# Two 128-byte spacers ahead of hh and hl, and two 128-row tiles in place of a transposed product for experts with 768 slots

## The chip, the cores and the metric

One NeuronCore of a Trainium2 chip runs the whole program. The metric is device time in microseconds (us), the median of several runs of the same program on the same inputs. A lower number is better.

## The reference

An attention layer (4 batches, 8 heads, 768 positions, head size 64; each query sees 8 global keys and the last 96 local ones) feeds a mixture of experts over N = 3072 tokens of width D = 512:

```python
logits = x @ w_gate
noisy = logits + np.log1p(np.exp(x @ w_noise)) * noise
top2 = two largest of noisy, weights by softmax over the two
for e in range(8):
    for k in range(2):
        mask = top2[:, k] == e
        h = np.maximum(x[mask] @ w1[e], 0.0)       # 512 -> 1024
        out[mask] += top2_w[mask, k, None] * (h @ w2[e])   # 1024 -> 512
```

Each expert therefore takes some 768 of the 6144 token-expert pairs, with two dense products per pair. All of it is float32.

## The kernel before

The program has two halves. The first (about 190 us) is the attention with the gate and the routing of tokens; the change does not reach it. The second is the experts, one after another, in the order of their token counts. Expert number e (0 to 7) has `CAPS[e]` slots: 812, 812, 804, 792, 780, 768, 768, 768. The first `CA = 512` slots of an expert are called part 0 here, the remaining 300, 292, 280, 268 or 256 are part 1.

A float32 product is made from three products of the faster type float32r: every operand is split into a high part and a low part (`xh`/`xl`, `w1h`/`w1l`, `w2h`/`w2l`, `hh`/`hl`), and high·high, high·low and low·high are added up in PSUM. For one expert the steps are:

- `up(e, c, f)` (L841): for part c and each of the 8 blocks f of 128 hidden units, 12 matmuls (4 blocks of the 512 inputs, three products each). The weights w1 stand still in the array, the tokens x move: 512 columns for part 0, 256 to 300 for part 1. ScalarE then writes `hh` with a Relu (L845) and VectorE writes `hl` (L846).
- `down(e, t)` (L868): for each of the 4 tiles t of 128 slots of part 0, 24 matmuls (8 blocks f, three products). Here 128 columns of hh or hl stand still, and a row of 512 columns of w2 moves; the result has slots as rows and goes straight to `put`, which scales it on ScalarE (L852) and adds it to the output by a scattered DMA that GpSimd issues (L853).
- `down_t(e, d)` (L879): part 1 is done the other way round, because its length is not a multiple of 128. For each of 4 blocks d of the outputs, 24 matmuls with w2 standing still and the 256 to 300 slots of part 1 moving. The result is transposed, so it goes to `yt` (L882, L884), and
- `back(e, t)` (L892) transposes it with 4 matmuls for every 128 slots, before `put`. The `back` steps of expert e are issued inside `up` of expert e + 1, behind the blocks f = 0, 1, 2; those of the last expert stand behind its tiles 0, 1, 2.

Beside these steps stand, for the next expert, `gather` (L180, fetches 128 token rows by an indirect DMA), `turn` (L230, 4 transposing matmuls for such a tile, then copies to xh and xl) and `split` (L158, L159, ScalarE and VectorE cut w1 into its parts). The order is written by hand. In the stage of the products with w2, the list `steps + steps_t` (4 `down`, then 4 `down_t`) is run through, and behind step j come split j and turn j of the next expert. For the last expert the list is `steps_t + steps`.

The tiles of the pool `mc` lie behind one another in each partition of SBUF: w2h and w2l (16384 bytes each), xh1 and xl1 (4 rows of 1200 bytes each), then hh in two tiles (part 0: 8 rows of 2048 bytes, part 1: 8 rows of 1200), hl in two such tiles, and yt. By these sizes hh begins 42368 bytes behind w2h, which is 384 more than a multiple of 512, and hl begins 68352 behind it, 256 more than a multiple of 512. In the pool `wts`, w1h, w1l, xh and xl of part 0 lie whole multiples of 512 bytes apart.

Of the kernel before, what the change touches and what calls it, by code (L numbers as in the profile page):

```python
# [10 lines left out]
F32 = mybir.dt.float32  # L11
# [5 lines left out]
AF = mybir.ActivationFunctionType  # L17
# [3 lines left out]
P = 128  # L21
NP = 96
TA = 4
TB = 3
CA = TA * P
# [3 lines left out]
CAPS = [812, 812, 804, 792, 780, 768, 768, 768]  # L29
# [5 lines left out]
def tile_local_global_attention_then_moe(  # L35
# [13 lines left out]
    nc = tc.nc  # L49
# [100 lines left out]
    def split(e, x, j, eng=nc.vector):  # L150

        t = raw[x, e, j // 4]
        if x == 1:
            t = t[:, :, (j % 4) * P:(j % 4 + 1) * P]
            hi, lo = (y[:, :, j * P:(j + 1) * P] for y in (w1h, w1l))
        else:
            t, hi, lo = t[:, j % 4], w2h[:, j], w2l[:, j]
        nc.scalar.activation(hi, t, AF.Copy)  # L158
        eng.tensor_sub(lo, t, hi.bitcast(F32))  # L159
        if j % 4 == 3 and (e or x == 2):  # L160
            load_w()
# [3 lines left out]
    def tiles(e):  # L165
        return -(-CAPS[e] // P)
# [657 lines left out]
    with ExitStack() as mctx:  # L824
        mc = mctx.enter_context(tc.tile_pool(name="mc", bufs=1))
        mw = mctx.enter_context(tc.tile_pool(name="mw", bufs=2))
        w2h = mc.tile([P, FC, Dm], FR, name="w2h")
        w2l = mc.tile([P, FC, Dm], FR, name="w2l")
        xh.append(mc.tile([P, KC, CB], FR, name="xh1"))
        xl.append(mc.tile([P, KC, CB], FR, name="xl1"))  # L830
        hh = [mc.tile([P, FC, n], FR, name=f"hh{n}") for n in (CA, CB)]
        hl = [mc.tile([P, FC, n], FR, name=f"hl{n}") for n in (CA, CB)]
        yt = mc.tile([P, KC, CB], F32, name="yt")
        def up(e, c, f, between=None):
            m = CAPS[e] - CA if c else CA
            ps = bank("sc" if f % 2 else "at")[:, :m]
            fs = slice(f * P, (f + 1) * P)
            n = 0
            for k in range(KC):
                for w, x in ((w1h, xh), (w1h, xl), (w1l, xh)):  # L840
                    nc.tensor.matmul(ps, w[:, k, fs], x[c][:, k, :m], start=n == 0, stop=n == 3 * KC - 1)  # L841
                    n += 1
                    if between and n % 3 == 0:
                        between()
            nc.scalar.activation(hh[c][:, f, :m], ps, AF.Relu)  # L845
            nc.vector.scalar_tensor_tensor(hl[c][:, f, :m], ps, 0.0, hh[c][:, f, :m].bitcast(F32),  # L846
                                           op0=OP.max, op1=OP.subtract)

        def put(e, t, ps):
            r, g = rows(e, t)  # L850
            y = mw.tile([r.shape[0], Dm], F32, name="y")
            nc.scalar.activation(y, ps, AF.Copy, scale=g)  # L852
            ins = nc.gpsimd.indirect_dma_start(  # L853
                out=out, out_offset=bass.IndirectOffsetOnAxis(ap=r, axis=0),
                in_=y, in_offset=None, bounds_check=N + DUMP - 1, oob_is_err=True, compute_op=OP.add)
            for o in added[e]:
                tc.declare_no_dep(ins.ins, o.ins, reason="an expert's tokens are all different")
            added[e].append(ins)

        added = [[] for _ in range(E)]  # L860

        def down(e, t):
            ps = bank("av")
            cols = slice(t * P, (t + 1) * P)
            n = 0
            for f in range(FC):
                for x, w in ((hh, w2h), (hh, w2l), (hl, w2h)):
                    nc.tensor.matmul(ps, x[0][:, f, cols], w[:, f], start=n == 0, stop=n == 3 * FC - 1)  # L868
                    n += 1
            put(e, t, ps)  # L870

        def down_t(e, d):
            m = CAPS[e] - CA
            ps = bank("av")[:, :m]
            cols = slice(d * P, (d + 1) * P)
            n = 0
            for f in range(FC):
                for w, x in ((w2h, hh), (w2h, hl), (w2l, hh)):
                    nc.tensor.matmul(ps, w[:, f, cols], x[1][:, f, :m], start=n == 0, stop=n == 3 * FC - 1)  # L879
                    n += 1  # L880
            if d % 2:
                nc.vector.tensor_copy(yt[:, d, :m], ps)  # L882
            else:
                nc.scalar.activation(yt[:, d, :m], ps, AF.Copy)  # L884

        def back(e, t):
            m = min(P, CAPS[e] - CA - t * P)
            if m <= 0:
                return
            ps = spare_bank()[:m]  # L890
            for d in range(KC):
                nc.tensor.transpose(ps[:, d * P:(d + 1) * P], yt[:, d, t * P:t * P + m], ident)  # L892
            put(e, TA + t, ps)

        late, last = pending
        slots = {
            0: [(late, 33)], 1: [gate_t, (late, 36)], 2: [(late, 39)], 3: [gate_l, (late, 42)],
            4: [], 5: [gate_s, (late, 45)], 6: [(last, 2)], 7: [(late, 48)],  # L900
            8: [(last, 5)], 9: [(last, 7)], 10: [(late, 52), (last, 8)], 11: [(last, 9)],
            12: [(last, 12)], 13: [(late, 54), (last, 13)], 14: [(last, 16)], 15: [(last, 18)],
            16: [(last, 20)], 17: [(last, 22)], 18: [(last, 24)], 19: [(last, 27)],
            20: [(last, 31)], 21: [(late, 57)], 22: [(last, 34)], 23: [(last, 37)],
            24: [(last, 39)], 25: [(last, 42)], 26: [(late, 61)], 27: [(last, 45)],
            28: [(last, 48)], 29: [(late, 99), split], 30: [split], 31: [(last, 52)],
        }
        slot, parts = [0], [0]

        def ahead():  # L910
            for x in slots[slot[0]]:
                if x is split:
                    split(0, 2, parts[0])
                    parts[0] += 1
                elif isinstance(x, tuple):
                    x[0].upto(x[1])
                elif windowed:
                    x(NT - 1)
            slot[0] += 1

        for f in range(FC):
            if NZ + f < (DUMP + N) // P // 2:
                zero_out(NZ + f)
            up(0, 0, f, ahead)
        while parts[0] < FC:
            split(0, 2, parts[0])
            parts[0] += 1
        for x in pending:
            x.upto(99)
        for t in range(TB):  # L930
            gather(0, TA + t)
        rank()
        ranked[0] = None
        load_w(held[0])
        for t in range(TA - 1):
            down(0, t)
        for t in range(TB):
            turn(0, TA + t, bank("sc") if t == TB - 1 else None)
        for t in range(3):
            gather(1, t)  # L940
        down(0, TA - 1)
        for e in range(E):
            last = e + 1 == E
            for c in range(2):
                if c or e:
                    for f in range(FC):
                        up(e, c, f)
                        if f % 2 and e:
                            split(e, 2, c * 4 + f // 2)
                        if c == 0 and f < TB:  # L950
                            back(e - 1, f)
                        if e == 0 and f % 2 and f < 6:
                            turn(1, f // 2)
                            gather(1, 3 + f // 2)
                if e and not last:
                    for t in range(3 * c, 3 + 2 * c):
                        gather(e + 1, t)
            steps = [(down, t) for t in range(TA)]
            steps_t = [(down_t, d) for d in range(KC)]
            if e == 0:  # L960
                for j in range(KC):
                    down_t(0, j)
                    if j == 0:
                        gather(1, 6)
                    turn(1, 3 + j)
                    split(1, 1, 2 * j)
                    split(1, 1, 2 * j + 1)
                continue
            for j, (f, t) in enumerate(steps_t + steps if last else steps + steps_t):
                f(e, t)  # L970
                if not last:
                    split(e + 1, 1, j)
                    if j < TA + TB:
                        turn(e + 1, j)
                        if j < 2:
                            gather(e + 1, 5 + j)
                elif j in (KC, KC + 1, KC + 2):
                    back(e, j - KC)


# [107 lines left out]
```

## Time and profile before

| | |
|---|---|
| median of 3 runs | 793.47 us (792.6 to 795.06) |
| the profiled execution: its own time | 789.53 us |
| its span, first to last instruction | 787.8 us |
| mean granted TensorE clock | 0.996 |
| TensorE matmuls busy | 771.5 us, 98% of the span, 5673 instructions |
| VectorE, ScalarE, GpSimd busy | 42%, 42%, 24% |

Matmuls are pipelined: one that the profile gives 0.39 us overlaps the next, so the time that a stream of them takes is read from their starts. Where the text speaks of a pace, it is the distance between two starts. A weight load stands in the profile as an instruction of its own, beside the matmul before it.

### The profile page before, as it was taken

How to read it: one execution, taken by the hardware profiler on the slowest of the kernel's cores; microseconds unless marked ns; L12 is line 12 of the kernel's file. 1: busy time of each engine (PE TensorE's matmuls, PEld its weight loads, DVE VectorE, ACT ScalarE, POOL GpSimd, SP SyncE). 2: the span in 40 equal slices, each digit the busy share in tenths (PEclk: the TensorE clock that was granted, in tenths of full speed). 3: DMA queues.
4: the chain of work that ended last, by engine and by line, in shares of the span. 5: the costliest groups of instructions: out<-in, count | busy, mean ns of one | idle time of the engine just before them, and what ended most of it. 6: DMA issues, size and time to landing. Idle time of an engine off the chain costs nothing.

```text
span 787.8 us, 14898 instructions
## 1 busy us (share of the span) xinstructions
PE 771.5 (98%) x5673; PEld 680.9 (86%) x5673; DVE 329.9 (42%) x1215; ACT 332.7 (42%) x726; POOL 192.3 (24%) x222
## 2 busy tenths in 40 slices
PE   7999999999999999999999999999999999999994
PEld 6989989898879989898888889898989889898983
DVE  6557566758853433233323422342334234233400
ACT  6778777765223433233333323342333323233310
POOL 2003431452035050404122321402051221211022
PEclk9999999999999999999999999999999999999998
DMA  8789675744256163344444434434453454432024
GB/s 267 241 271 315 191 204 168 220 147 151 104 156 175 56 150 108 57 126 97 117 84 103 129 83 93 108 95 97 104 123 109 64 136 122 94 81 27 2 28 58
DMA packets 58786, 99.67 MB, mean 127 GB/s; under 512 B 5076, under 2 KB 17492, under 8 KB 58704
## 3 DMA queue, kind: packets, MB, share of 16 engines
q1 hardware_dynamic: 47440, 72.79, 28.8%
q0 software_dynamic: 11264, 25.83, 18.2%
q8 instruction: 47, 0.77, 0.4%
q14 instruction: 35, 0.29, 0.1%
HBM read 71.01 MB, written 27.59 MB: 125 GB/s over the span
## 4 chain that ended last, share of the span: by engine, by line
PE 63%; issue 28%; POOL 6%; DMA 1%; POOLq 0%; DVE 0%; ACT 0%; SPq 0%
PE av L868 11%; PE sc L841 10%; PE at L841 10%; PE av L661 9%; PE av L879 7%; PE at L641 6%; PE sc L613 5%; POOL out_dram L853 4%; POOL xg L180 2%; PE m L252 1%; PE m L260 1%; PE m L230 1%; PE lg L230 1%; PE lg L426 1%; DMA out_dram<-y,ids 1%
## 5 line engine op out<-in xcount | busy, mean ns | idle before, releaser
L853 POOL DMA_INDIRECT out_dram<-y,ids x53 | 83.1, 1567 | 405.1 <-ACT y L852 404.1
L868 PE MATMUL av<-w2h,hh 128*128 128x512 f32 x256 | 102.6, 401 | 0.0
L868 PE MATMUL av<-w2h,hl 128*128 128x512 f32 x256 | 101.5, 396 | 0.0
L868 PE MATMUL av<-w2l,hh 128*128 128x512 f32 x256 | 101.2, 395 | 0.0
L159 DVE TENSOR_TENSOR w1l<-raw,w1h 128x512 fp32r<-128x512 f32 x56 | 38.3, 689 | 144.0 <-ACT w1h L158 144.0
L841 PE MATMUL sc<-xh,w1h 128*128 128x512 f32 (+5 forms) x256 | 88.3, 345 | 0.0
L841 PE MATMUL at<-xh,w1h 128*128 128x512 f32 (+5 forms) x256 | 88.3, 345 | 0.0
L841 PE MATMUL at<-xl,w1h 128*128 128x512 f32 (+5 forms) x256 | 87.1, 340 | 0.1
L841 PE MATMUL sc<-xh,w1l 128*128 128x512 f32 (+5 forms) x256 | 87.1, 340 | 0.0
L841 PE MATMUL at<-xh,w1l 128*128 128x512 f32 (+5 forms) x256 | 87.1, 340 | 0.0
L841 PE MATMUL sc<-xl,w1h 128*128 128x512 f32 (+5 forms) x256 | 87.0, 340 | 0.0
L846 DVE SCALAR_TENSOR_TENSOR hl<-sc,hh 128x512 fp32r<-128x512 f32 (+5 forms) x64 | 36.3, 568 | 97.0 <-ACT hh L845 97.0
L879 PE MATMUL av<-hh,w2h 128*128 128x256 f32 (+4 forms) x256 | 76.1, 297 | 0.0
L629 ACT ACTIVATE a<-ns,mx 128x168 f32<-128x168 f32 (+1 forms) x192 | 71.9, 422 | 6.4 <-POOL a L543 4.2
L879 PE MATMUL av<-hh,w2l 128*128 128x256 f32 (+4 forms) x256 | 74.1, 290 | 0.0
L879 PE MATMUL av<-hl,w2h 128*128 128x256 f32 (+4 forms) x256 | 74.1, 290 | 0.0
L845 ACT ACTIVATE hh<-sc 128x512 fp32r<-128x512 f32 (+5 forms) x64 | 32.0, 500 | 99.8 <-PE sc L841 99.8
L852 ACT ACTIVATE y<-av,tab 128x512 f32<-128x512 f32 x28 | 19.2, 687 | 127.2 <-issue 106.4
L180 POOL DMA_INDIRECT xg<-xd,ids x53 | 56.5, 1066 | 59.9 <-DVE place L200 38.7
L661 PE MATMUL av<-vs,at 128*128 128x65 f32 x384 | 70.9, 273 | 0.0
L845 ACT ACTIVATE hh<-at 128x512 fp32r<-128x512 f32 (+5 forms) x64 | 32.0, 500 | 86.9 <-PE at L841 86.8
L643 ACT ACTIVATE at<-at 128x512 f32<-128x512 f32 (+1 forms) x96 | 53.6, 558 | 29.6 <-PE at L641 29.2
(163 smaller groups left out, 1572.3 us busy)
## 6 DMA issues: line engine op xcount, KB each, us to landing
raw<-in_w SPq DMA_DIRECT2D x32, 1024.0 KB, 5.3
out_dram<-zero SPq DMA_DIRECT2D x14, 512.0 KB, 5.6
vs<-in_v SPq DMA_DIRECT2D x24, 260.0 KB, 4.0
qbuf<-in_q SPq DMA_DIRECT2D x24, 256.0 KB, 5.5
xd<-xr SPq DMA_DIRECT2D x24, 256.0 KB, 2.5
ks<-in_k SPq DMA_DIRECT2D x20, 272.0 KB, 4.3
vp<-in_v SPq DMA_DIRECT2D x20, 195.0 KB, 4.8
ks<-in_k SPq DMA_DIRECT2D x4, 464.0 KB
```

Source lines behind the costliest of these rows:

```text
L159: eng.tensor_sub(lo, t, hi.bitcast(F32))
L180: nc.gpsimd.indirect_dma_start(out=xg[e, t], out_offset=None, in_=xd[:n], in_offset=bass.IndirectOffsetOnAxis(ap=r, axis=0), bounds_check= ...
L613: nc.tensor.matmul(SC[n + x][y * Q:(y + 1) * Q, s], qs[b, j][r, 2 * i0 + s, u + y], ks[b, j][r, u + y, k0:k0 + w], start=True, stop=True, ...
L629: nc.scalar.activation(A[n][:, s, c:c + w], ns[:, s, :w], AF.Exp, bias=mx[:, s:s + 1], scale=-1.0)
L641: nc.tensor.transpose(p4[:, :, c, s * Q:(s + 1) * Q], x[:, s, a:a + P], ident)
L643: nc.scalar.activation(AT[n], ps, AF.Copy)
L661: nc.tensor.matmul(ps[:, h % 4], a[:kk, y * w + c0:y * w + c0 + P], t[:kk, c], start=kk < P or not i, stop=kk == P)
L841: nc.tensor.matmul(ps, w[:, k, fs], x[c][:, k, :m], start=n == 0, stop=n == 3 * KC - 1)
L845: nc.scalar.activation(hh[c][:, f, :m], ps, AF.Relu)
L853: ins = nc.gpsimd.indirect_dma_start(out=out, out_offset=bass.IndirectOffsetOnAxis(ap=r, axis=0), in_=y, in_offset=None, bounds_check=N + ...
L868: nc.tensor.matmul(ps, x[0][:, f, cols], w[:, f], start=n == 0, stop=n == 3 * FC - 1)
L879: nc.tensor.matmul(ps, w[:, f, cols], x[1][:, f, :m], start=n == 0, stop=n == 3 * FC - 1)
```

## The change

Two tiles of 32 float32 (128 bytes in each partition) are allocated ahead of hh and ahead of hl and never used. They move hh by 128 bytes and hl, yt and y by 256. By the sizes above, hh then begins 42496 bytes behind w2h and hl 68608, both whole multiples of 512.

For an expert whose part 1 is a whole number of 128-slot tiles (`whole_tiles`: experts 5, 6 and 7, with 256 slots there), hh and hl of part 1 are written and read with rows of 256 floats (1024 bytes) in place of 300 (`second`), `down` does two more tiles (t = 4, 5) with these as the standing operand, and `down_t` and `back` are left out. The splits and turns of the next expert are spread over the six steps that remain.

```diff
+        mc.tile([P, 32], F32, name="pad0")
         hh = [mc.tile([P, FC, n], FR, name=f"hh{n}") for n in (CA, CB)]
+        mc.tile([P, 32], F32, name="pad1")
         hl = [mc.tile([P, FC, n], FR, name=f"hl{n}") for n in (CA, CB)]
...
-            nc.scalar.activation(hh[c][:, f, :m], ps, AF.Relu)
+            hi, lo = (second(x[c], e) if c else x[c] for x in (hh, hl))
+            nc.scalar.activation(hi[:, f, :m], ps, AF.Relu)
...
+        def whole_tiles(e):
+            return (CAPS[e] - CA) % P == 0
+        def second(x, e):
+            if not whole_tiles(e):
+                return x
+            m = CAPS[e] - CA
+            return x.rearrange("p f t -> p (f t)")[:, :FC * m].rearrange("p (f t) -> p f t", f=FC)
...
         def down(e, t):
             ps = bank("av")
-            cols = slice(t * P, (t + 1) * P)
+            c, a = (0, t * P) if t < TA else (1, (t - TA) * P)
+            cols = slice(a, a + P)
+            hi, lo = (second(x[c], e) if c else x[c] for x in (hh, hl))
             n = 0
             for f in range(FC):
-                for x, w in ((hh, w2h), (hh, w2l), (hl, w2h)):
-                    nc.tensor.matmul(ps, x[0][:, f, cols], w[:, f], start=n == 0, stop=n == 3 * FC - 1)
+                for x, w in ((hi, w2h), (hi, w2l), (lo, w2h)):
+                    nc.tensor.matmul(ps, x[:, f, cols], w[:, f], start=n == 0, stop=n == 3 * FC - 1)
...
-            if m <= 0:
+            if m <= 0 or whole_tiles(e):
                 return
...
+            if whole_tiles(e):
+                steps, steps_t = [(down, t) for t in range(tiles(e))], []
...
-                    split(e + 1, 1, j)
-                    if j < TA + TB:
-                        turn(e + 1, j)
-                        if j < 2:
-                            gather(e + 1, 5 + j)
+                    while parts * len(steps) < FC * (j + 1):
+                        split(e + 1, 1, parts)
+                        turn(e + 1, parts)
+                        if parts < 2:
+                            gather(e + 1, 5 + parts)
+                        parts += 1
```

On TensorE, in the w2 stage of expert 5, the end of tile 3 and what follows it read before (hh_3633 and hl_3635 are part 0, hh_3634 and hl_3636 part 1; xg is a gathered tile of the next expert):

```order
L868 MATMUL av<-w2l,hh_3633 128x512
L868 MATMUL av<-w2h,hl_3635 128x512
L230 MATMUL m<-ident,xg 128x128 x4
L879 MATMUL av<-hh_3634,w2h 128x256
L879 MATMUL av<-hl_3636,w2h 128x256
L879 MATMUL av<-hh_3634,w2l 128x256
```

and in the changed program (hh_3634 and hl_3637 are part 0 there, hh_3635 and hl_3638 part 1):

```order
L884 MATMUL av<-w2l,hh_3634 128x512
L884 MATMUL av<-w2h,hl_3637 128x512
L230 MATMUL lg<-ident,xg 128x128 x4
L230 MATMUL m<-ident,xg 128x128 x4
L884 MATMUL av<-w2h,hh_3635 128x512
L884 MATMUL av<-w2l,hh_3635 128x512
L884 MATMUL av<-w2h,hl_3638 128x512
```

Two turns now stand together, and the products that follow have 512 moving columns; there are 48 of them in place of 96 with 256 columns.

On TensorE again, in `up` of expert 6, at the border of blocks f = 0 and f = 1, before:

```order
L841 MATMUL at<-xl_99,w1h 128x512
L841 MATMUL at<-xh_98,w1l 128x512
L892 MATMUL lg<-ident,yt 128x128 x4
L841 MATMUL sc<-xh_98,w1h 128x512
L841 MATMUL sc<-xl_99,w1h 128x512
```

and in the changed program:

```order
L843 MATMUL at<-xl_99,w1h 128x512
L843 MATMUL at<-xh_98,w1l 128x512
L843 MATMUL sc<-xh_98,w1h 128x512
L843 MATMUL sc<-xl_99,w1h 128x512
L843 MATMUL sc<-xh_98,w1l 128x512
```

The four transposes of `back` are gone from there, and from behind the next block too.

On ScalarE, from tile 3 of expert 5 (its y) to the start of `up` of expert 6 (hh_3633 there), before:

```order
L852 ACTIVATE y<-av,tab 128x512
L158 ACTIVATE w1h<-raw 128x4x128
L232 ACTIVATE xh_98<-m 128x4x128
L884 ACTIVATE yt<-av 128x256
L158 ACTIVATE w1h<-raw 128x4x128
L232 ACTIVATE xh_3631<-lg 128x4x128
L158 ACTIVATE w1h<-raw 128x4x128
L232 ACTIVATE xh_3631<-m 128x4x128
L884 ACTIVATE yt<-av 128x256
L158 ACTIVATE w1h<-raw 128x4x128 x2
L845 ACTIVATE hh_3633<-at 128x512
L852 ACTIVATE y<-lg,tab 128x512
```

and in the changed program:

```order
L855 ACTIVATE y<-av,tab 128x512
L158 ACTIVATE w1h<-raw 128x4x128
L232 ACTIVATE xh_3631<-lg 128x4x128
L158 ACTIVATE w1h<-raw 128x4x128
L232 ACTIVATE xh_3631<-m 128x4x128
L855 ACTIVATE y<-av,tab 128x512
L158 ACTIVATE w1h<-raw 128x4x128
L855 ACTIVATE y<-av,tab 128x512
L158 ACTIVATE w1h<-raw 128x4x128
L848 ACTIVATE hh_3634<-at 128x512
L848 ACTIVATE hh_3634<-sc 128x512
```

The copies to yt and the y of `back` are replaced by the y of tiles 4 and 5; the turns of the next expert end one step after tile 3 in place of two.

## Rows read from the trace of the kernel before

**Rows 1.** Busy time by engine in the expert half (240 to 776.5 us); granted clock, DMA.

```profile
core 0: us, PE busy (x) PEld busy (x) DVE busy (x) ACT busy (x) POOL busy (x), PEclk, DMA share, GB/s
240.00:776.50 536.50, 536.50 (x3158) 475.39 (x3156) 175.46 (x308) 177.76 (x343) 125.53 (x95) 1.00 0.40 93
```

**Rows 2.** TensorE groups by line and shape, two of them: count, busy, mean.

```profile
L868 PE MATMUL av<-w2h,hh 128*128 128x512 f32 x256 | 102.6, 401 | 0.0
...
L879 PE MATMUL av<-hh,w2h 128*128 128x256 f32 x96 | 27.4, 286 | 0.0
```

**Rows 3.** Timeline of TensorE (start us, length us, what), `up` of expert 1, part 0.

```profile
286.86 0.39 PE L841 MATMUL sc<-xh,w1h 128*128 128x512 f32 x1
...
292.30 0.39 PE L841 MATMUL sc<-xh,w1h 128*128 128x512 f32 x1
```

**Rows 4.** Timeline of TensorE, `down` of expert 0, first matmuls of tiles 1 and 2.

```profile
223.83 0.39 PE L868 MATMUL av<-w2h,hh 128*128 128x512 f32 x1
...
229.43 0.39 PE L868 MATMUL av<-w2h,hh 128*128 128x512 f32 x1
```

**Rows 5.** Timeline of TensorE, `up` of part 1: expert 1 (300 columns), expert 6 (256).

```profile
295.02 0.30 PE L841 MATMUL at<-xh,w1h 128*128 128x300 f32 x1
...
308.26 0.39 PE L868 MATMUL av<-w2h,hh 128*128 128x512 f32 x1
...
660.48 0.28 PE L841 MATMUL at<-xh,w1h 128*128 128x256 f32 x1
...
671.78 0.40 PE L868 MATMUL av<-w2h,hh 128*128 128x512 f32 x1
```

**Rows 6.** Timeline of TensorE, w2 stage of expert 5, to the start of expert 6.

```profile
601.43 0.40 PE L868 MATMUL av<-w2h,hh 128*128 128x512 f32 x1
...
607.02 0.60 PE L230 MATMUL lg<-ident,xg 128*128 128x128 f32 x4
...
613.41 0.48 PE L868 MATMUL av<-w2h,hh 128*128 128x512 f32 x1
...
619.09 0.60 PE L230 MATMUL lg<-ident,xg 128*128 128x128 f32 x4
619.44 0.48 PE L868 MATMUL av<-w2h,hh 128*128 128x512 f32 x1
...
637.72 0.40 PE L841 MATMUL at<-xh,w1h 128*128 128x512 f32 x1
```

**Rows 7.** Timeline of TensorE, `up` of expert 7, blocks f = 2 and f = 4.

```profile
714.39 0.47 PE L841 MATMUL at<-xh,w1h 128*128 128x512 f32 x1
...
719.95 0.39 PE L841 MATMUL at<-xh,w1h 128*128 128x512 f32 x1
```

**Rows 8.** Timeline of TensorE, `up` of expert 6, blocks f = 0 and f = 3.

```profile
640.49 0.60 PE L892 MATMUL lg<-ident,yt 128*128 128x128 f32 x4
...
646.88 0.39 PE L841 MATMUL sc<-xh,w1h 128*128 128x512 f32 x1
```

**Rows 9.** Timeline of TensorE, w2 stage of expert 7, first to last matmul.

```profile
742.14 0.28 PE L879 MATMUL av<-hh,w2h 128*128 128x256 f32 x1
...
753.39 0.39 PE L868 MATMUL av<-w2h,hh 128*128 128x512 f32 x1
...
776.43 0.40 PE L868 MATMUL av<-w2h,hl 128*128 128x512 f32 x1
```

**Rows 10.** Timeline of all engines, the end of the program.

```profile
776.91 0.69 ACT L852 ACTIVATE y<-av,tab 128x512 f32<-128x512 f32 x1 [4.87 <-PE av L868]
777.87 1.57 POOL L853 DMA_INDIRECT out_dram<-y,ids  x1 [3.99 <-ACT y L852]
```

**Rows 11.** Instructions that write xg, 560 to 720 us: the gathers, their landing.

```profile
DMA to landing us min/median/max: 3.5/3.7/4.3
```

**Rows 12.** Timeline of TensorE, expert 5, two slow neighbours within the first tile.

```profile
603.51 0.40 PE L868 MATMUL av<-w2h,hh 128*128 128x512 f32 x1
...
603.99 0.39 PE L868 MATMUL av<-w2h,hl 128*128 128x512 f32 x1
```

More of the change, by code (lines that the diff above doesn't have):

```diff
@@ L844, in up @@
                         between()
-            nc.scalar.activation(hh[c][:, f, :m], ps, AF.Relu)
-            nc.vector.scalar_tensor_tensor(hl[c][:, f, :m], ps, 0.0, hh[c][:, f, :m].bitcast(F32),
+            hi, lo = (second(x[c], e) if c else x[c] for x in (hh, hl))
+            nc.scalar.activation(hi[:, f, :m], ps, AF.Relu)
+            nc.vector.scalar_tensor_tensor(lo[:, f, :m], ps, 0.0, hi[:, f, :m].bitcast(F32),
                                            op0=OP.max, op1=OP.subtract)
@@ L968, in tile_local_global_attention_then_moe @@
                 continue
-            for j, (f, t) in enumerate(steps_t + steps if last else steps + steps_t):
+            if whole_tiles(e):
+                steps, steps_t = [(down, t) for t in range(tiles(e))], []
+            steps = steps_t + steps if last else steps + steps_t
+            parts = 0
+            for j, (f, t) in enumerate(steps):
                 f(e, t)
                 if not last:
-                    split(e + 1, 1, j)
-                    if j < TA + TB:
-                        turn(e + 1, j)
-                        if j < 2:
-                            gather(e + 1, 5 + j)
-                elif j in (KC, KC + 1, KC + 2):
+                    while parts * len(steps) < FC * (j + 1):
[4 more added lines that the diff above has]
+                        parts += 1
+                elif steps_t and j in (KC, KC + 1, KC + 2):
                     back(e, j - KC)
```

## The prediction

> **What bounds the kernel.** I read the busy times of the expert half first, then the starts of TensorE's matmuls. In the 536.5 us from 240 to 776.5 TensorE is busy for all 536.50, at a granted clock of 1.00, while VectorE and ScalarE work a third of that and the DMA engines are at 0.40 [rows 1]. So in this half time goes only where the stream of matmuls gets shorter, and whatever leaves VectorE, ScalarE or GpSimd is worth nothing by itself. The attention half is not touched.
>
> A matmul's length in the profile (401 ns for the 256 of one `down` product [rows 2]) is no pace, since neighbours overlap. The starts give it. In `up` of part 0, 24 matmuls of 512 columns take 292.30 - 286.86 = 5.44 us, 226.7 ns each [rows 3]. In `down`, 24 matmuls of 512 columns take 229.43 - 223.83 = 5.60 us, 233.3 ns each [rows 4]. The shape is the same, and so is the pattern of three products (two matmuls with the high weights, one with the low, moving high, low, high), and neither stream has a gap. What differs is where the operands lie. In `up`, w1h, w1l, xh and xl lie whole multiples of 512 bytes apart; in `down`, hh and hl lie 384 and 256 bytes off that grid against w2. The streams of part 1 give a second hint, as their rows are 1200 bytes apart and fall off the grid too: 96 matmuls of 300 columns take 13.24 us (137.9 ns each), 96 of 256 take 11.30 us (117.7 ns) [rows 5]. A line through these two, 0.459 ns for each column, reaches 235 ns at 512 columns. `down` lies on that line (233.3); `up` of part 0 alone lies 8 ns below it. My theory: the standing operand that is being loaded and the row that is moving get in each other's way a little, depending on their relative place, and 512-byte steps are the good case. No trace here shows the same stream at two places, so this is the step that I choose.
>
> **The change part by part.** The spacers put hh and hl on the 512-byte grid against w2, part 1's tiles included, and rows of 1024 bytes keep the new tiles there.
>
> 1. Pace of `down`, experts 0 to 4. The gain per matmul is bounded by nothing and by the 6.7 ns between [rows 4] and [rows 3]; below nothing is the third rival. I take 6.7, the row with the same shape and pattern. It isn't reached at once. A tile of `down` behind a turn takes 619.09 - 613.41 = 5.68 us [rows 6]; 24 matmuls of `up` behind a `back` take 719.95 - 714.39 = 5.56 [rows 7]. That is 0.12 us per such tile. The first tile of an expert, entered from a narrower stream, takes 607.02 - 601.43 = 5.59 [rows 6]; `up`'s first block, entered so, takes 640.49 - 637.72 = 2.77 for 12 [rows 6, 8] where 2.72 is the steady value, so 24 would take 5.49, 0.10 less. Expert 0: two undisturbed tiles at 0.16, two at 0.12, **0.56 us**. Experts 1 to 4: 0.10 + 3 x 0.12 = 0.46 each, **1.84 us**.
>
> 2. The w2 stage of experts 5 and 6. Before it runs from 601.43 to 637.72, 36.29 us [rows 6]. After: tile 0 at 5.49, tiles 1 to 4 behind a turn at 5.56, tile 5 undisturbed at 5.44, in all 33.17. Six turns remain, each 619.44 - 619.09 = 0.35 us [rows 6]. They now stand as two, one, one, two. A pair without a product between it loses some overlap: at least 2 x 0.35 = 0.70, at most 0.60 (the length of a set of four) + 0.35 = 0.95; I take 0.79, nearer the lower end. That makes 2 x 0.79 + 2 x 0.35 = 2.28. The stage is 35.45, so 0.84 less, **1.68 us** for both. The exchange of 96 narrow for 48 wide matmuls is itself nearly even (11.3 us for 96 [rows 5] against 48 x 226.7 ns = 10.9).
>
> 3. `back` of experts 5 and 6 goes. Three blocks of `up` of expert 6 with two `back` sets take 646.88 - 637.72 = 9.16 us [rows 6, 8]; three blocks undisturbed are 3 x 2.72 = 8.16. For experts 6 and 7 together **2.00 us**.
>
> 4. Expert 7. Its stage runs from 742.14 to the last matmul's start at 776.43, 34.29 us [rows 9], two `back` sets between its tiles included. After, it is 144 matmuls without any disturbance: 143 x 226.7 ns + 0.05 for the entry = 32.47. **1.82 us**.
>
> 5. The end: from the last matmul to the end of the span 787.8 - 776.43 = 11.4 us, one y and one scattered DMA [rows 10]. The same steps follow tile 5, so nothing.
>
> 6. `down_t` of experts 0 to 4 keeps its form, but its moving rows shift by 128 or 256 bytes. Two placements of a 256-column stream differ by 0.5 ns (117.7 [rows 5]; 753.39 - 742.14 over 96 = 117.2 [rows 9]), and 480 such matmuls make 0.3 us either way. I take nothing.
>
> 7. Covers. ScalarE loses the copies to yt and the scaling of `back` and gains two y per expert, VectorE likewise: nothing, as both have two thirds of the time free [rows 1]. Behind tiles 0 and 3 ScalarE now has five pieces at once (y, two splits, two turns); a y is 0.69 us [rows 10], so some 3.5 us against a tile of 5.5, and the splits must only be there before `up`'s blocks 6 and 7. On GpSimd's queue the gather of the next expert's tile 5 still follows turn 0 and the scatter of tile 0; its turn now comes behind tile 3, some 18 us later in place of 24, and it lands in 3.5 to 4.3 us [rows 11]. The number of scatters and gathers is unchanged.
>
> The sum is 0.56 + 1.84 + 1.68 + 2.00 + 1.82 = 7.9 us. The profiled execution (789.53 us) would become 781.6. The median of the runs is 793.47, 0.5% above that execution; a difference of matmul time carries over as it is, so the forecast is **785.6 us** (-1.0%).
>
> **Rivals.** *The spacers do nothing.* Then only steps 2 to 4 are left, at 233.3 ns: experts 5 and 6 at 5.59 + 4 x 5.68 + 5.60 + 2.28 = 36.19, 0.1 us less each; 2.0 for `back`; expert 7 at 143 x 233.3 = 33.36, 0.93 less. That is 3.1 us, 790.4. For it: the two paces might belong to the products and not to the addresses. Against it: same shape and pattern, no gap in either, and the line through part 1. The Trainium skill speaks for this rival: "TensorE: Matmul & The Clock Gate", section "Step-by-step: what each phase is for", says that loading the next weights takes no read bandwidth from the running matmul, and "SBUF — State Buffer", section "Who interferes with whom", that PE never waits on anyone. By that rule the place of an operand can't matter and 790.4 is the time. This trace does not settle it, but the rule leaves the 6.7 ns between the two streams without a cause.
>
> *Half of it.* If only one of the two moved operands mattered, or the good pace were often lost, the 912 `down` matmuls (768 and 144 new ones) would gain about half: 5.5 us, 788.0. For it speaks that the good pace takes about ten matmuls to settle; against it that after that `up` doesn't lose it.
>
> *Worse: the new place is a bad one.* If hh, hl and w2 on one grid hinder each other, every `down` matmul gets slower. The slowest neighbours in a tile now are 603.99 - 603.51 = 0.48 us for two, 240 ns [rows 12]. 912 x 6.7 ns = 6.1 us lost against 3.1 gained gives 796.5. It decides from 3.4 ns per matmul on (236.7). Against it: `up` holds 226.7 on just such a grid.
>
> **How the numbers follow.** Forecast 0.74, spacers without effect 0.14, half 0.07, worse 0.05. A measurement of this kernel tells about 0.3% from no change, 2.4 us here. The forecast and the half case are faster by more than that. The case without effect lies at 0.39%, so I count 0.09 of its 0.14 as faster and 0.05 as the same. Of the worse case 0.02 is the same and 0.03 slower. That gives 0.90 faster, 0.07 the same, 0.03 slower. The forecast's own range is 783.6 to 787.6: about 0.3 for `down_t`, 0.2 for the pairs of turns, up to 1 for how soon the pace settles, and the runs themselves, which spread from 0.9 below to 1.6 above their median. The range goes from 783.4 to 790.9, which takes in the half case and most of the case without effect, and leaves out the worse one and the edges.
>
> **What would show it.** Step 1: `down` tiles in which 24 starts span 5.44 us once settled, and 5.56 behind a turn; if they still span 5.60 and 5.68, the theory of places is wrong. Step 2: 35.4 to 35.5 us from expert 5's first `down` to expert 6's `up`. Step 3: 8.16 us for three blocks there. Step 4: 32.5 us from the first to the last w2 matmul. An idle gap of TensorE behind the paired turns, or a wait for a gather there, would refute step 7; a slower `down_t` would show in experts 0 to 4 alone.

## The result and the profile after

The median of six runs is 784.32 us (783.33 to 787.53) against 794.26 us for six runs of the kernel before; the ratio is 0.9887, with a 95% interval from 0.9864 to 0.9909. The change is faster, by 1.1%, and the time lies 1.3 us below the forecast of 785.6 and inside both ranges. The profiled execution took 783.56 us. Whole runs of one kernel also differ by the mean clock that TensorE was granted (of the kernel below with everything on the grid, six runs at 0.984 took 791.3 to 794.6 us and six at 0.995 or more 783.5 to 784.8), so medians compare two kernels only roughly.

Its span, and the busy time of each engine:

```profile
span 781.8 us, 14552 instructions
PE 764.4 (98%) x5505; PEld 671.7 (86%) x5505; DVE 327.6 (42%) x1209; ACT 330.4 (42%) x720; POOL 192.7 (25%) x222
```

The expert half by stretch, as in [rows 1], from 240 us to the last matmul; one group of the `down` products by shape, which stands in [rows 2] for before:

```profile
240.00:770.40 530.40, 530.40 (x2996) 467.04 (x2994) 174.31 (x305) 176.19 (x339) 127.40 (x96) 1.00 0.41 96
```

```profile
L884 PE MATMUL av<-w2h,hh 128*128 128x512 f32 x304 | 120.4, 396 | 0.0
```

TensorE is busy for every one of those 530.40 us, still at a granted clock of 1.00, so the time went where matmuls are: there are 168 fewer of them (5673 - 5505), and the 304 of a kind that now stand in place of 256 are each closer to the next. The timeline of TensorE (start us, length us, what) shows both. First, two undisturbed tiles of expert 0, the w2 stage of expert 5 with its first pair of turns, and three blocks of `up` of expert 6:

```profile
225.43 0.39 PE L884 MATMUL av<-w2h,hh 128*128 128x512 f32 x1
...
230.87 0.39 PE L884 MATMUL av<-w2h,hh 128*128 128x512 f32 x1
...
600.90 0.39 PE L884 MATMUL av<-w2h,hh 128*128 128x512 f32 x1
...
606.38 0.60 PE L230 MATMUL lg<-ident,xg 128*128 128x128 f32 x4
606.82 0.60 PE L230 MATMUL m<-ident,xg 128*128 128x128 f32 x4
607.17 0.48 PE L884 MATMUL av<-w2h,hh 128*128 128x512 f32 x1
...
636.34 0.39 PE L843 MATMUL at<-xh,w1h 128*128 128x512 f32 x1
...
644.50 0.39 PE L843 MATMUL sc<-xh,w1h 128*128 128x512 f32 x1
```

A tile takes 230.87 - 225.43 = 5.44 us, where [rows 4] had 5.60. The stage runs 636.34 - 600.90 = 35.44 us, where [rows 6] had 36.29. The three blocks run 644.50 - 636.34 = 8.16 us, where [rows 6, 8] had 9.16. Then the w2 stage of expert 7, first to last matmul, and the end of the program:

```profile
737.94 0.39 PE L884 MATMUL av<-w2h,hh 128*128 128x512 f32 x1
...
770.40 0.39 PE L884 MATMUL av<-w2h,hl 128*128 128x512 f32 x1
770.87 0.69 ACT L855 ACTIVATE y<-av,tab 128x512 f32<-128x512 f32 x1 [4.75 <-PE av L884]
```

That is 32.46 us in place of 34.29 [rows 9], and 781.8 - 770.4 = 11.4 us behind it as before [rows 10].

The two profiled executions are 6.0 us apart, less than the steps add up to, because the attention half, which the change doesn't reach, took 1.6 us longer in the second. Its end is the first matmul of `up` of expert 0, before and after:

```profile
192.60 0.47 PE L841 MATMUL at<-xh,w1h 128*128 128x512 f32 x1
```

```profile
194.24 0.48 PE L843 MATMUL at<-xh,w1h 128*128 128x512 f32 x1
```

From there to the last matmul the expert half takes 776.43 - 192.60 = 583.83 us before and 770.40 - 194.24 = 576.16 after, 7.67 us less. The medians of six runs are 9.9 us apart; their interval, 7.2 to 10.8 us, takes in the 7.67, and no stage shows the rest. The start of the expert half moved between 192.5 and 199.2 us over the profiles of this study, in kernels with the same attention half, while stages that a kernel left alone came out mostly equal to 0.02 us. So below, single executions are compared by their stages and not by their whole time.

### The profile page after: what moved, and what is told of

The parts are those of the page before. It is cut to its first block, busy times and chain, and to the rows that moved or that the text cites. A ratio compares the mean times of both kernels' runs of the same rounds, so it can differ in the third digit from the quotient of the medians.

```text
span 781.8 us, 14552 instructions
## 1 busy us (share of the span) xinstructions
PE 764.4 (98%) x5505; PEld 671.7 (86%) x5505; DVE 327.6 (42%) x1209; ACT 330.4 (42%) x720; POOL 192.7 (25%) x222
## 4 chain that ended last, share of the span: by engine, by line
PE 81%; issue 14%; POOL 3%; DMA 1%; DVE 0%; POOLq 0%; ACT 0%; SPq 0%
PE av L884 18%; PE sc L843 14%; PE at L843 14%; PE av L661 9%; PE av L895 8%; PE at L641 6%; PE sc L613 5%; POOL out_dram L856 2%; PE m L252 1%; PE m L230 1%; PE m L260 1%; PE lg L230 1%; PE lg L426 1%; DMA out_dram<-y,ids 1%; PE lg L267 1%
## 5 line engine op out<-in xcount | busy, mean ns | idle before, releaser
L884 PE MATMUL av<-w2h,hh 128*128 128x512 f32 x304 | 120.4, 396 | 0.0
L884 PE MATMUL av<-w2h,hl 128*128 128x512 f32 x304 | 118.8, 391 | 0.0
L884 PE MATMUL av<-w2l,hh 128*128 128x512 f32 x304 | 118.6, 390 | 0.0
L855 ACT ACTIVATE y<-av,tab 128x512 f32<-128x512 f32 x34 | 23.4, 688 | 146.7 <-issue 115.7
L884 PEld LDWEIGHTS av<-w2h,hl 128*128 128x128 f32 x304 | 57.1, 188 | 12.1
L884 PEld LDWEIGHTS av<-w2l,hh 128*128 128x128 f32 x304 | 57.2, 188 | 11.4 <-DVE w2l L159 0.3
L884 PEld LDWEIGHTS av<-w2h,hh 128*128 128x128 f32 x304 | 57.1, 188 | 11.0
```

The lines of the kernel that those rows point to most:

```text
L884: nc.tensor.matmul(ps, x[:, f, cols], w[:, f], start=n == 0, stop=n == 3 * FC - 1)
```

## The experiments

The theory on record was that a standing operand and a moving row hinder each other by their relative place, and that multiples of 512 bytes are the good case. Its rival was that place doesn't matter. Below, two operands lie on the grid when they are a whole multiple of that step apart, and off it by the bytes that are left over.

### The tiles without the spacers

```diff
-        mc.tile([P, 32], F32, name="pad0")
-        mc.tile([P, 32], F32, name="pad1")
```

> The change without the two spacers: hh and hl lie where they lay before, 384 and 256 bytes off the 512-byte grid of w2. If the place of the operands sets the pace of the down products, a settled tile of 24 matmuls takes 5.60 us again and one behind a turn 5.68; the w2 stage of expert 5 takes 36.2 us, that of expert 7 33.4, three blocks of up of expert 6 still 8.16; the time is 3.1 us below the kernel before (ratio 0.996). If the place doesn't matter and the pace came with the new order, everything is as with the change: 5.44 and 5.56, 35.45 and 32.46, ratio 0.989.

790.06 us against 792.5 before, ratio 0.9961 (0.9926 to 0.9996). From the timeline of TensorE, the w2 stage of expert 5 up to block 3 of the next `up`, then that of expert 7 with one of its undisturbed tiles:

```profile
606.69 0.40 PE L882 MATMUL av<-w2h,hh 128*128 128x512 f32 x1
...
642.87 0.39 PE L841 MATMUL at<-xh,w1h 128*128 128x512 f32 x1
...
651.03 0.39 PE L841 MATMUL sc<-xh,w1h 128*128 128x512 f32 x1
...
745.21 0.40 PE L882 MATMUL av<-w2h,hh 128*128 128x512 f32 x1
...
750.80 0.39 PE L882 MATMUL av<-w2h,hh 128*128 128x512 f32 x1
...
756.40 0.39 PE L882 MATMUL av<-w2h,hh 128*128 128x512 f32 x1
...
778.57 0.40 PE L882 MATMUL av<-w2h,hl 128*128 128x512 f32 x1
```

The stage takes 36.18 us, the three blocks 8.16, the last stage 33.36, the tile 5.60. The expert half is 580.72 us long, 3.1 below before, as steps 2 to 4 give without the better pace. The instructions are those of the change, in its order; only the addresses differ, and the pace went back to 233.3 ns. So the spacers do it, and the rival falls.

### The spacers without the tiles

```diff
+        mc.tile([P, 32], F32, name="pad0")
         hh = [mc.tile([P, FC, n], FR, name=f"hh{n}") for n in (CA, CB)]
+        mc.tile([P, 32], F32, name="pad1")
```

> The kernel before with the two spacers and nothing else. If the place sets the pace, all 32 down tiles take 5.44 us settled and 5.56 behind a turn, about 3.9 us less in all (ratio 0.995), and the transposed product and back take what they took. If place doesn't matter, the time is that of the kernel before (ratio 1.000) and the tiles take 5.60 and 5.68.

788.76 us against 792.5, ratio 0.9969 (0.994 to 0.9998). From the timeline of TensorE, two starts in expert 0, and the transposed product of expert 6:

```profile
225.41 0.39 PE L870 MATMUL av<-w2h,hh 128*128 128x512 f32 x1
...
230.85 0.39 PE L870 MATMUL av<-w2h,hh 128*128 128x512 f32 x1
...
694.45 0.36 PE L881 MATMUL av<-hh,w2h 128*128 128x256 f32 x1
...
706.81 0.39 PE L843 MATMUL at<-xh,w1h 128*128 128x512 f32 x1
```

The tiles reach 5.44 us, and over the eight experts `down` gets 3.66 us shorter (23.95 to 23.50 us for expert 0, some 0.45 for each of the next six, 23.03 to 22.51 for expert 7). But the expert half shrank by 3.27 us only, to 580.56, not by 3.9: the transposed product of experts 5 to 7 got longer, 12.36 us here against 12.24 for expert 6, together 0.37. Its moving rows lie elsewhere by 128 bytes (hh) and 256 (hl). The change doesn't meet this, since it drops that product for these three.

### Offsets by expert

One tile holds hh and hl of part 0, and each expert writes and reads them there at an offset of its own, so that one execution compares eight places.

```diff
+        part0 = mc.tile([P, 2 * FC * CA + 80], FR, name="part0")
+        AT0 = [(0, n, n) for n in (0, 0, 8, 16, 32, 48, 64, 80)]
...
+            swap, a, b = AT0[e]
+            x, y = (part0[:, o:o + FC * CA].rearrange("p (f t) -> p f t", f=FC) for o in (a, FC * CA + b))
+            return (y, x) if swap else (x, y)
```

> The change with hh and hl of part 0 at an offset to w2's grid that differs by expert, the same for both: 0, 0, 32, 64, 128, 192, 256, 320 bytes for experts 0 to 7; part 1 of experts 5 to 7 stays on the grid. If only whole multiples of 512 are good, experts 0 and 1 settle at 226.7 ns a matmul, all the others at 233 or so. If the pace falls off with the distance, the offsets lie between, 32 and 64 nearer to 226.7. If what counts is that hh and hl lie alike, and not how they lie to w2, all experts settle at 226.7. Tiles 4 and 5 of experts 5 to 7 settle at 226.7 under each of these.

From the timeline of TensorE, the 15th and the 24th matmul of a tile, nine starts apart, in the first tile of experts 2 (32 bytes), 4 (128), 5 (192), 6 (256) and 7 (320):

```profile
390.13 0.40 PE L892 MATMUL av<-w2h,part 128*128 128x512 f32 x1
392.22 0.39 PE L892 MATMUL av<-w2h,part 128*128 128x512 f32 x1
...
537.19 0.39 PE L892 MATMUL av<-w2h,part 128*128 128x512 f32 x1
539.28 0.39 PE L892 MATMUL av<-w2h,part 128*128 128x512 f32 x1
...
608.48 0.39 PE L892 MATMUL av<-w2h,part 128*128 128x512 f32 x1
610.54 0.40 PE L892 MATMUL av<-w2h,part 128*128 128x512 f32 x1
...
677.11 0.39 PE L892 MATMUL av<-w2h,part 128*128 128x512 f32 x1
679.15 0.39 PE L892 MATMUL av<-w2h,part 128*128 128x512 f32 x1
...
751.28 0.40 PE L892 MATMUL av<-w2h,part 128*128 128x512 f32 x1
753.38 0.39 PE L892 MATMUL av<-w2h,part 128*128 128x512 f32 x1
```

With the trace's nanoseconds these nine starts give, in ns a matmul (off the grid the distances alternate, so the expert's other tiles differ from its first by up to 0.7):

| offset, bytes | 0 | 32 | 64 | 128 | 192 | 256 | 320 |
|---|---|---|---|---|---|---|---|
| pace | 226.7 | 233.1 | 233.7 | 231.9 | 228.9 | 226.7 | 233.7 |

Every offset here holds hh and hl alike to each other, and most are slow, so it is the place against w2 that counts. But 256 bytes are as good as 0. The grid on record was too coarse: it is 256 bytes, not 512. The pace doesn't fall off with the distance either; 32 bytes cost all there is. Tiles 4 and 5 of experts 5 to 7, which stay on the grid, settle at 226.7 in the same execution, for expert 7 right behind tiles at 233.7.

### Which of the two operands

Against the run before, only the offsets change.

```diff
-        AT0 = [(0, n, n) for n in (0, 0, 8, 16, 32, 48, 64, 80)]
+        AT0 = [(0, 0, 0), (0, 0, 0), (0, 0, 32), (1, 0, 32), (0, 32, 32), (0, 0, 64), (1, 0, 64), (0, 64, 64)]
```

> The same, with offsets (hh, hl) of part 0 by expert: (0,0), (0,0), (0,128), (128,0), (128,128), (0,256), (256,0), (256,256) bytes. If each standing operand is hindered by the row that moves meanwhile, an expert with one of them off the grid loses a part that goes with the number of its matmuls: hh stands in two of three products, hl in one, so (128,0) loses about twice what (0,128) does, and (128,128) all 6.7 ns. If one operand off the grid spoils the whole rhythm, all but (0,0) settle at 233. If hh and hl must lie alike, (128,128) and (256,256) settle at 226.7 and the mixed ones don't.

The same two matmuls of a tile, for experts 2 (hl off by 128) and 3 (hh off by 128), and the paces of all:

```profile
389.13 0.40 PE L892 MATMUL av<-w2h,part 128*128 128x512 f32 x1
391.21 0.40 PE L892 MATMUL av<-w2h,part 128*128 128x512 f32 x1
...
463.05 0.40 PE L892 MATMUL av<-w2h,part 128*128 128x512 f32 x1
465.15 0.40 PE L892 MATMUL av<-w2h,part 128*128 128x512 f32 x1
```

| hh, hl off by (bytes) | 0, 0 | 0, 128 | 128, 0 | 128, 128 | 0, 256 | 256, 0 | 256, 256 |
|---|---|---|---|---|---|---|---|
| pace, ns | 226.7 | 231.1 | 233.3 | 231.8 | 226.7 | 226.7 | 226.7 |

All three cases with 256 are good, which settles the grid. Of the three theories none fits whole. hh alone costs all 6.7 ns and hl alone 4.4, not one third of the sum, and both together cost less than hh alone. So the loss is no sum over the standing operands, one by one; it goes with the rhythm that the stream falls into, and what sets that rhythm is not shown. The kernel before had hh off by 384 and hl by 256 bytes, which on a grid of 256 is the case (128, 0): 233.3 ns, and here the same pattern of starts came back, 232, 233, 235 ns in turn. Seen so, hl was on the grid before the change and its move won nothing: the whole gain in pace is that of hh. The second spacer is needed to keep hl there when the first moves it by 128.

### Everything 64 bytes further

```diff
+        mc.tile([P, 16], F32, name="pad2")
         w2h = mc.tile([P, FC, Dm], FR, name="w2h")
```

> The change with 64 more bytes ahead of w2h, so that w2, hh and hl move together and keep their places to one another. If only the place of the standing operand to the moving row counts, settled down products stay at 226.7 ns a matmul and the w2 stage of expert 7 at 32.5 us. If the place of a tile in SBUF by itself counts, they leave 226.7, towards 233 (33.4 us).

From the timeline of TensorE, the same two matmuls in the second tile of expert 7:

```profile
749.41 0.39 PE L885 MATMUL av<-w2h,hl 128*128 128x512 f32 x1
...
751.45 0.39 PE L885 MATMUL av<-w2h,hl 128*128 128x512 f32 x1
```

Nine starts take 2.04 us, 226.7 ns each, and the stage 32.46 us, as with the change. So for the settled 512-column products the place in SBUF by itself doesn't count at these 64 bytes, only that of the operands to one another. One stream did change its pace: `up` of part 1, whose tokens (xh1, xl1) moved by the 64 bytes while w1 didn't, went from 137.9 to 137.3 ns at 300 columns and from 123.3 to 123.9 at 268. The runs with offsets hold xh1 at that same place to w1, and give these same two paces.

### Finer offsets

```diff
-        AT0 = [(0, n, n) for n in (0, 0, 8, 16, 32, 48, 64, 80)]
+        AT0 = [(0, n, n) for n in (0, 4, 12, 24, 40, 56, 60, 72)]
```

> As the run with offsets by expert, with 0, 16, 48, 96, 160, 224, 240, 288 bytes for experts 0 to 7, hh and hl alike. If the grid is 256 bytes and its period too, 288 gives the pace of 32 (233.4 ns), and 240 and 224 fall from the 228.9 of 192 towards the 226.7 of 256, while 16 and 48 lie at 233 like 32 and 64. If a wider grid played a part, 288 would differ from 32.

The same two matmuls for two tiles of expert 1 (16 bytes off), and for expert 7 (288):

```profile
310.71 0.39 PE L892 MATMUL av<-w2h,part 128*128 128x512 f32 x1
312.75 0.39 PE L892 MATMUL av<-w2h,part 128*128 128x512 f32 x1
...
316.68 0.39 PE L892 MATMUL av<-w2h,part 128*128 128x512 f32 x1
318.79 0.39 PE L892 MATMUL av<-w2h,part 128*128 128x512 f32 x1
...
747.11 0.40 PE L892 MATMUL av<-w2h,part 128*128 128x512 f32 x1
749.21 0.40 PE L892 MATMUL av<-w2h,part 128*128 128x512 f32 x1
```

288 gives 233.4 ns and 32 gave 233.1. Nearly every place off the grid lies near 233, so that alone says little; but the single distances come back too (about 232 and 235 ns in turn at 32 and 288, about 231 and 236 at 64 and 320), which fits a period of 256 bytes. Between, 48, 96, 160 and 224 bytes lie at 233 to 234, so the 228.9 of 192 is a dip of its own, and my guess of a fall towards 256 was wrong. At 16 bytes the same operands run at 226.7 in two tiles of an expert and at 233 in the two others; at 240 they run at 226.7 or 228.4. Near the grid both rhythms are possible. What chooses between them isn't shown: the tiles differ in what ran before them, and also in their place by multiples of 512 bytes.

### The narrow streams

The line through part 1 was a reason of the prediction: these rows lie off the grid, so their streams should be slow ones and gain on it. Two kernels put them there. The first moves the tokens of part 1 of experts 5 to 7 to rows of 1024 bytes; the second makes rows of 1280 bytes for all of part 1 and needs no spacers.

```diff
+            th, tl = (tokens(xh[1], e, 0), tokens(xl[1], e, 80)) if c else (xh[0], xl[0])
```

> The change, and for experts 5 to 7 the tokens xh and xl of part 1 too with rows of 1024 bytes on the grid of w1 (before: rows of 1200 bytes, off it). If the place law holds for a 256-column stream in the same proportion (226.7 ns for 512 columns), up of part 1 falls from 117.7 to 113.3 ns a matmul, 10.9 us in place of 11.3 for each of these experts. If what is left over the columns is a fixed 13 ns per matmul, it comes to 120 and 11.5 us. If a narrow stream is set by the weight loads, it stays at 117.7.

```diff
+CP = -(-CB // 64) * 64
...
-        hh = [mc.tile([P, FC, n], FR, name=f"hh{n}") for n in (CA, CB)]
+        hh = [mc.tile([P, FC, n], FR, name=f"hh{n}") for n in (CA, CP)]
...
-            y = mw.tile([r.shape[0], Dm], F32, name="y")
+            y = gp.tile([P, H, D], F32, name="xr", bufs=2).rearrange("p h d -> p (h d)")[:r.shape[0]]
```

> No spacers; rows of part 1 of xh, xl, hh and hl are 1280 bytes in place of 1200 (a multiple of 256), so that every operand of the experts lies on a 256-byte grid; y takes the two buffers of xr, which are free by then, to make the room. If 256 bytes are the grid, down products stay at 226.7 ns. If the law holds for the narrower streams in proportion, up and the transposed product of part 1 fall by 4.2 to 4.9 ns a matmul (300 columns: 137.9 to 132.8), 5.7 us below the change (ratio to the kernel before 0.981). If a fixed 13 ns per matmul is left, 300 columns take 138.3, 256 take 120, and the time is about 1 us above the change (0.990). If the grid is 512 after all, the down products go back to 233.

Timeline of TensorE, `up` of part 1 from its first matmul to the first of what follows, 96 matmuls. For the change, expert 7 (256 columns):

```profile
726.64 0.28 PE L843 MATMUL at<-xh,w1h 128*128 128x256 f32 x1
...
737.94 0.39 PE L884 MATMUL av<-w2h,hh 128*128 128x512 f32 x1
```

For the second of the two kernels, experts 1 (300 columns), 4 (268) and 7 (256):

```profile
296.57 0.30 PE L841 MATMUL at<-xh,w1h 128*128 128x300 f32 x1
...
309.69 0.39 PE L882 MATMUL av<-w2h,hh 128*128 128x512 f32 x1
...
518.12 0.28 PE L841 MATMUL at<-xh,w1h 128*128 128x268 f32 x1
...
529.64 0.39 PE L882 MATMUL av<-w2h,hh 128*128 128x512 f32 x1
...
726.75 0.28 PE L841 MATMUL at<-xh,w1h 128*128 128x256 f32 x1
...
738.26 0.40 PE L882 MATMUL av<-w2h,hh 128*128 128x512 f32 x1
```

On the grid, 256 columns take 11.51 us in both kernels, 119.9 ns a matmul against 117.7: slower, as the fixed remainder of the expectation would have it (226.7 ns at 512 columns and 119.9 at 256 lie 0.417 ns a column apart, which leaves 13.1 over). 300 columns take 13.12 us, 136.7 ns against 137.9, and 268 columns 11.52 in place of 11.84, 120.0 ns; neither the proportion (132.8 for the 300) nor the fixed remainder (138.3) fits those. Nor is 120.0 the price of 268 columns on the grid: the transposed product of expert 4 settles at 124.4 ns there. The `down` tiles stay at 5.44 us without spacers. By the sizes of the tiles, hh and hl of part 0 then begin 43008 and 69632 bytes behind w2h, multiples of 512 as well, so this run, other than its expectation has it, can't tell the two grids apart; the runs with offsets do. Taken together the second kernel's expert half is 575.97 us long against 576.16, which is no gain to speak of over the change; its ratio to before, 0.993 (0.9892 to 0.9968), is over runs at both clocks.

The last kernel keeps rows of 1200 bytes for the tokens of experts 5 to 7.

```diff
+        return x[1].rearrange("p k t -> p (k t)")[:, :KC * CB].rearrange("p (k t) -> p k t", k=KC)
```

> The run with everything on the grid, but the tokens of part 1 of experts 5 to 7 keep rows of 1200 bytes. By the stages of that run, up of part 1 takes 11.3 us again for these three (11.5 there), and 13.1, 12.8, 12.3 and 11.5 us for experts 1 to 4 (13.24, 12.89, 12.37, 11.84 with the change); the expert half is 0.8 us shorter than with the change, 575.4 us. If it is the 256-column stream's rows alone that matter, nothing else moves; a difference of 0.1% is below what the runs tell, so it stands in the stages alone.

`up` of part 1 of expert 7 takes 11.40 us there (725.52 to 736.92 in the timeline), between 11.30 and 11.51. There xl begins on the grid though its rows leave it, and its place to w1 is all that differs from the change for that stream. The expert half is 575.69 us, 0.5 below the change in place of 0.8. The time is 782.51 us against 790.28, ratio 0.9906 (0.9892 to 0.9919), which can't be told from the change's.

## Why the prediction was right, point by point

| step | forecast, us | in the profile, us |
|---|---|---|
| 1. `down` of expert 0 | 0.56 | 0.45 |
| 1. `down` of experts 1 to 4 | 1.84 | 1.80 |
| 2. w2 stage of experts 5 and 6 | 1.68 | 1.65 |
| 3. `up` of experts 6 and 7 | 2.00 | 2.00 |
| 4. w2 stage of expert 7 | 1.82 | 1.83 |
| 6. `down_t` of experts 0 to 4 | 0, within 0.3 | -0.03 |
| expert half | 7.9 | 7.67 |

Step 1 was right in mechanism and nearly in size: a tile settles at 5.44 us, and behind a turn takes 5.55 to 5.58 in experts 1 to 4 where 5.56 was taken. Only expert 0 fell short by 0.1: its first tile holds a distance of 0.33 us before and after, and gained 0.04 us (5.72 to 5.68) where 0.12 was taken. Step 2's pair of turns was the one value chosen between bounds, and 607.17 - 606.38 = 0.79 us is what it cost; with bounds of 0.70 and 0.95 an exact hit is luck. Step 5 held (11.4 us), and in step 7 no gap appeared: TensorE is busy throughout, and the turns of the pairs run without a wait in sight. By its stages the change is 0.2 us smaller than forecast, and yet the median is 1.3 us below the forecast. No stage accounts for that; it lies within the runs' spread (0.9887 of 793.47 is 784.5, with an interval from 782.7 to 786.2).

Two reasons were less good than the result. First, the grid. The prediction read multiples of 512 bytes off `up`; the offsets show 256. That gave the right answer here by luck, because 0 is on both grids, but a reader who put the hl of this kernel off by 256 to save room would have lost nothing, and the prediction would have said otherwise. Second, the line through part 1, which I used against the rival that the spacers do nothing. It reached 235 ns at 512 columns and matched `down`, but putting those narrow streams on the grid moved them by -3.3 to +2.2 ns and not along that line. It was a coincidence. What carried the forecast was the comparison of two streams alike in shape, pattern and absence of gaps.

The rival without effect fell by the run without spacers (790.06 us, 0.9961, where it would have had the change's own time): 32 bytes of displacement of the standing operands alone take a matmul from 226.7 to 233.1 ns. With it falls what was drawn from the pages beside it, that the place of an operand can't matter: the Trainium skill's "SBUF — State Buffer", section "Who interferes with whom", has PE waiting on no one, and "TensorE: Matmul & The Clock Gate", section "Step-by-step: what each phase is for", has weight loads taking no read bandwidth from the running matmul. Whether it is a load that takes the time, no run here shows. The rival of a half gain had two conditions. One came true, as only hh's move mattered, but its price was wrong: with hh alone off the grid the whole 6.7 ns are lost. The other, that the good pace is lost often, did not: in `down` it isn't lost once settled, until the next turn. The worse case would have needed 236.7 ns; no place that was tried settled above 233.9.

What stays open is why 256 bytes, and why hh off the grid costs more than hh and hl off it together. That the standing operand's load and the moving row are what collide fits the runs at 512 columns, but no run took one of them away, and it doesn't say why 256 columns in `up` got slower on the grid.

## What to carry to other kernels

Where two matmul streams of the same shape run at different paces without gaps, compare the places of their operands before anything else: with 512 float32r columns, standing and moving operands that lie a multiple of 256 bytes apart ran up to 3% faster here than at most other places, for 256 bytes of padding in each partition. Don't extend that to other widths unmeasured; at 256 columns the same placing made `up` slower. And a transposed product that needs transposing back costs its own matmuls and also those it interrupts: `back` was worth 1 us an expert, of which its two sets of transposes are 0.7.

## What the runs showed of the hardware that was not expected

- The grid is 256 bytes: 0 and 256 give 226.7 ns, 32 and 288 give 233.1 and 233.4, 64 and 320 both 233.7.
- Streams of the same instructions can run in two rhythms. At 16 bytes off the grid, two of an expert's four tiles ran at 226.7 ns and two at 233.
- A narrow stream follows another rule, which stays open: in `up`, 256 columns took 117.7 ns off the grid and 119.9 on it, 268 columns 123.3 off it and 120.0 on it.
- The attention half ended between 192.5 and 199.2 us in kernels that hardly differ there. In four of the eleven profiled executions TensorE's granted clock fell to 0.50 (1.2 GHz) for 3 to 7 us there, and these four ended it late, at 196.4 to 199.2 us. The row, as in [rows 1], is from the run without spacers, where TensorE had been busy for 0.78 us of the two just before. In the changed program's own profile it was busy for 0.98 of the same two, and the clock stayed at 1.00. One more ended late, at 197.3, without such a fall.

```profile
186.00:190.00 4.00, 4.00 (x22) 4.00 (x21) 1.28 (x9) 2.85 (x7) 0.00 (x0) 0.50 0.32 104
```
